# The order of TensorE's work inside a slot of a banded-attention and MLP kernel

## The chip, the cores and the metric

The kernel runs on one core of a Trainium2 chip. The metric is the device time of one execution in microseconds (us). Three runs of the kernel before took 751.92 to 752.27 us, median 752.23.

## What is computed

The reference, cut to what matters (x has 2048 rows of 512; 32 heads of 16 columns; window 256; hidden width 1792):

```python
x = A_x
xn = _layernorm(x, axis=-1)
# attention
qkv = (xn @ wqkv).reshape(B, S, 3, H, Dh).transpose(2, 0, 3, 1, 4)
scores = jnp.einsum("bhqd,bhkd->bhqk", q, k) * (Dh ** -0.5)
mask = (i - j >= 0) & (i - j < 256)
p = _softmax(jnp.where(mask, scores, -1e9), axis=-1)
s = jnp.einsum("bhqk,bhkd->bhqd", p, v).transpose(...).reshape(B, S, D) @ wo
# MLP
y = _layernorm(xn, axis=-1)
g = silu(gelu(y @ w1 + b1) @ w2 + b2)
return x + s * g
```

All of it is in float32. Each operand of a large product is split into a high and a low float32r part, and three matmuls (high times high, high times low, low times high) take the place of one.

## The kernel before

The attention works on groups of four heads (`NQ` = 8 groups) and on 16 blocks of 128 keys in each group. The loop at line 819 runs over slots t; slots 0 to 127 handle one (group, key block) each, slots -16 to -1 prepare the first group, and the MLP follows. In slot t the kernel runs four kinds of work for different blocks at once, and all of TensorE's instructions stand in the order in which the loop writes them (`keep_in_program_order`; the same holds for VectorE, ScalarE and GpSimd).

- **Scores** of the slot's key block: `prob_block(n, kb, p)` (line 548), once for p = 1, which I call the first scores, and once for p = 0, the second scores. Two matmuls write up to 384 columns for two heads into the two banks of `stb`, which exists once. ScalarE takes the exponential of both banks into a tile `pt`, and GpSimd masks its two triangles (`affine_select`). The next scores can be written only when ScalarE has read the banks.
- **Maxima** of block m = t + 12 (`LEAD`): `max_block` (line 496). Four matmuls write the scores of a query block against two key blocks into `xy`. VectorE lays, by the triangular mask, the scores of the block two further back (in `zo`) over the upper triangles (`copy_predicated`), and takes the maximum (`tensor_reduce`).
- **First-block scores**: `first_scores` (line 487), the four matmuls into `zo` that this mask copy reads. With `ahead=True` in `max_block` they were issued in the slot before.
- **Values**: `pv_step(n, qb)` (line 569), up to 24 small matmuls of the probabilities of the slot before into `otb`, a part of one bank of `zo`, and ScalarE's copy of it into `oraw` (`outs["copy"]`).
- **Fills**: `fill_in(t, half)` (line 812) runs the units that are planned for the first half (0) or the second half (1) of the slot. They are projections for later groups and the first hidden units of the MLP. `tandem` (line 440) spreads two such products over slots t0 to t1: each unit is a pair of matmuls on the upper and the lower 64 rows into the two banks `fb`. In the middle the banks change rows; the first unit after that waits, by a manual dependency, for the latest `outs["copy"]`. At slot t1 ScalarE copies one bank and VectorE the other. `places` puts up to a third of the product's units of a slot into the first half (4 of 12 pairs of 512 columns, 8 of 24 of 256), what is over into the second half, and up to 3 (or 6) last ones into the first half of t1. `BEHIND` (line 438) lists eight t1 whose ScalarE copy is issued in the second half.

The loop's order for TensorE, and with it for all engines, is in lines 825 to 846: first scores, maxima, first-half fills, the plan's other steps, second scores, second-half fills, first-block scores of the next slot, values. The `plan` (`at`) and the `ends` (`behind`) of a slot carry the splits of weights, layernorm steps and DMA issues. SyncE issues all DMAs, in program order.

"Slot" below means a turn of this loop. VectorE's chain in a slot is mask copy, then maximum; the next block's four matmuls into `xy` must wait for that maximum. The mask copy also waits in the program for ScalarE's latest copy of `otb`, which lies in the same bank as `zo`.

Of the kernel before, what the change touches and what calls it, by code (L numbers as in the profile page):

```python
# [23 lines left out]
NQ = H // 4  # L24
EPS = 1e-5
NEG = -3.0e38
LEAD = 12
# [23 lines left out]
def mixer_kernel(ctx, tc, x, wqk, wv, wo, w1, b1, w2, b2, out):  # L51


    nc = SimpleNamespace(**{name: Ordered(tc, name) for name in ("tensor", "vector", "scalar", "gpsimd", "sync")})
# [105 lines left out]
    def run(steps):  # L160
        for step in steps:
            step()
# [13 lines left out]
    def open_slot(i):  # L176
        slots.append(bigp.tile([P, 2, 2, S], F32R, tag=f"qk{i}", name=f"qk{i}"))
# [18 lines left out]
    fb = [psf.tile([P, 512], F32, name=f"fb{i}") for i in range(2)]  # L196
# [90 lines left out]
    now = [0, 0]  # L287
    delayed = {}
    fills = {}

    def later(k, fn):

        if k == 0:
            fn()
        else:
            h = 2 * now[0] + now[1] + k
            delayed.setdefault((h // 2, h % 2), []).append(fn)
# [137 lines left out]
                behind(t, nc.sync.dma_start, h_d[f - 6], raw)  # L435
        return 3 * KT, mm, finish

    BEHIND = (19, 24, 35, 41, 58, 74, 90, 104)

    def tandem(t0, t1, one, two, mid=None, back=None):  # L440

        n = one[0]
        lo, hi = slice(0, 64), slice(64, P)
        mid = mid or max(1, (t0 + t1 + 1) // 2)
        most = n // 4

        def places(slots, last):

            last = min(most, n // (len(slots) + 1)) if last else 0
            cuts = [(n - last) * k // len(slots) for k in range(len(slots) + 1)]
            out = []
            for t, a, b in zip(slots, cuts, cuts[1:]):
                ahead = min(b - a, max(n // 3, (b - a + 1) // 2))
                out += [(t, 0)] * ahead + [(t, 1)] * (b - a - ahead)
            return out + [(t1, 0)] * last

        first, second = places(range(t0, mid), False), places(range(back or mid, t1), True)
        for phase, where in enumerate((first, second)):  # L460
            for i in range(n):
                flags = dict(start=(phase == 0 and i == 0), stop=(phase == 1 and i == n - 1), skip_group_check=True)
                def unit(i=i, phase=phase, flags=flags):
                    made = ((two if phase == 0 else one)[1](fb[1 - phase], i, hi, **flags),
                            (one if phase == 0 else two)[1](fb[phase], i, lo, **flags))
                    if phase == 1 and i == 0:
                        for r in made:
                            tc.add_manual_dep(r.ins, outs["copy"].ins.name, ORDER, reason="the banks change rows")
                fills.setdefault(where[i], []).append((unit, ()))
        fills.setdefault((t1, int(t1 in BEHIND)), []).append((one[2], (fb[0], t1, nc.scalar.copy)))  # L470
        fills[t1, 0].append((two[2], (fb[1], t1, nc.vector.tensor_copy)))

    def spread(jobs, places):
# [13 lines left out]
    def first_scores(n, qb):  # L487

        slot = slots[n % 2]
        for p in range(2):  # L490
            for a in (1, 0):
                r = slice(64 * a, 64 * a + 64)
                nc.tensor.matmul(zo[:, a, P * p: P * (p + 1)], slot[r, 0, p, P * qb: P * (qb + 1)],
                                 slot[r, 1, p, P * (qb - 2): P * (qb - 1)], start=True, stop=True)

    def max_block(n, qb, ahead=False):

        slot = slots[n % 2]
        if qb % 4 == 0:
            mts[n, qb // 4] = small.tile([P, 2, 2, 4], F32, tag="mt", name=f"mt_{n}_{qb}")  # L500
        lo = max(qb - 1, 0)
        off = 128 * (lo + 1 - qb)
        for p in range(2):
            for a in (1, 0):
                r = slice(64 * a, 64 * a + 64)
                nc.tensor.matmul(xy[:, a, 256 * p + off: 256 * (p + 1)], slot[r, 0, p, P * qb: P * (qb + 1)],
                                 slot[r, 1, p, P * lo: P * (qb + 1)], start=True, stop=True)
        if qb >= 2 and not ahead:
            first_scores(n, qb)
        four = xy.rearrange("q a (p k) -> q a p k", p=2)  # L510
        nc.vector.copy_predicated(four[:, :, :, 128:256], mask,
                                  neg if qb < 2 else zo[:, :, 0:256].rearrange("q a (p k) -> q a p k", p=2))
        nc.vector.tensor_reduce(out=mts[n, qb // 4][:, :, :, qb % 4],
                                in_=four[:, :, :, off:256],
                                axis=AX.X, op=ALU.max, negate=True)
# [32 lines left out]
    def prob_block(n, kb, p):  # L548
        slot = slots[n % 2]
        w = min(384, S - P * kb)  # L550
        pt = pp.tile([P, 2, 384], F32, tag="pt", name=f"pt_{n}_{kb}_{p}")
        both = xy if p and 16 * n + kb + LEAD >= 16 * NQ else stb[0]
        for a in (1, 0):
            r = slice(64 * a, 64 * a + 64)
            nc.tensor.matmul(both[:, a, 0:w], slot[r, 1, p, P * kb: P * (kb + 1)],
                             slot[r, 0, p, P * kb: P * kb + w], start=True, stop=True)
        nc.scalar.activation(pt[:, :, 0:w], both[:, :, 0:w], AF.Exp, scale=DH ** -0.5)
        nc.gpsimd.affine_select(out=pt[:, :, 0:P], in_=pt[:, :, 0:P], pattern=[[0, 2], [1, P]],
                                compare_op=ALU.is_ge, fill=0.0, base=0, channel_multiplier=-1)
        if w == 384:  # L560
            nc.gpsimd.affine_select(out=pt[:, :, 256:384], in_=pt[:, :, 256:384],
                                    pattern=[[0, 2], [-1, P]], compare_op=ALU.is_gt, fill=0.0,
                                    base=0, channel_multiplier=1)
        pts[(n, kb, p)] = pt
# [4 lines left out]
    def pv_step(n, qb):  # L569

        lo = max(qb - 2, 0)
        for kb in range(lo, qb + 1):
            for j in range(4):
                nc.tensor.matmul(otb[32 * j: 32 * j + DH + 1], vt[:, kb, (4 * n + j) % 16],
                                 pts[n, kb, j // 2][:, j % 2, P * (qb - kb): P * (qb - kb + 1)],
                                 start=(kb == lo), stop=(kb == qb),
                                 skip_group_check=True, tile_position=(0, 32 * j))
        if qb % 4 == 0:
            outs[0] = sgp.tile([P, 512], F32, tag="or", name=f"oraw_{n}_{qb}", bufs=2)
        outs["copy"] = nc.scalar.copy(outs[0][:, P * (qb % 4): P * (qb % 4 + 1)], otb)  # L580
        if qb % 4 == 3:
            (at if n or qb > 7 else behind)(16 * n + qb + 2, nc.sync.dma_start, oT_d[n // 2, n % 2::2, :, P * (qb - 3): P * (qb + 1)], outs[0])
# [82 lines left out]
    def at(t, fn, *args):  # L665
        plan.setdefault(t, []).append((fn, args))
# [145 lines left out]
    def fill_in(t, half):  # L812
        now[:] = t, half
        run(delayed.pop((t, half), ()))
        for fn, args in fills.get((t, half), ()):
            fn(*args)

    end = 16 * NQ
    for t in range(-16, end + 1):
        m = t + LEAD  # L820
        if t == -5:
            open_slot(1)
            for k in range(4):
                at(-4 + k, clear_part, k)
        if 0 <= t < end:
            if t == 0:
                early.close()
                stb.append(attn.enter_context(tc.tile_pool(name="ps_s2", bufs=1, space=PSUM)).tile(
                    [P, 2, 512], F32, name="stb"))
            prob_block(t // 16, t % 16, 1)  # L830
        if t >= 0 and m < end:
            max_block(m // 16, m % 16, t > 0)
        fill_in(t, 0)
        for fn, args in plan.get(t, []):
            fn(*args)
        if 4 <= m < LEAD:
            max_block(0, m)
        if 0 <= t < end:
            prob_block(t // 16, t % 16, 0)
        fill_in(t, 1)  # L840
        if 0 <= m < 4:
            max_block(0, m)
        if t >= 0 and m + 1 < end and (m + 1) % 16 >= 2:
            first_scores((m + 1) // 16, (m + 1) % 16)
        if t >= 1:
            pv_step((t - 1) // 16, (t - 1) % 16)
        run(lns.get(t, ()))
        if 0 <= m < end and m % 4 == 3:
            max_rows(m // 16, m % 16 // 4, t)
        for fn, args in ends.get(t, []):  # L850
            fn(*args)
# [22 lines left out]
    for f in range(6, NF, 2):  # L874
        t = gp.tile([P, 2, 512], F32, tag="ohl", name=f"hr_{f}", bufs=4)
# [429 lines left out]
```

## Time and profile before

| what | value |
|---|---|
| median of three runs | 752.23 us |
| the profiled execution | 751.99 us |
| its span, first to last instruction | 750.3 us |
| TensorE busy | 735.8 us (98%) |
| VectorE, ScalarE, GpSimd busy | 511.3, 439.5, 299.1 us |
| slots 0 to 127 | about 62 to 427 us of the span |
| granted TensorE clock | 0.999 |

In the profile PE is TensorE's matmuls and PEld its weight loads, which may run beside matmuls; DVE is VectorE, ACT ScalarE, POOL GpSimd, SP SyncE. A row of the timeline gives start and duration in us, engine, line, operation, output <- inputs, shape, and in brackets the idle time before it with what ended it. All operations go through one recording helper and so have the line L43; they are told apart by their tiles. A matmul's duration includes the latency of the array, so busy times of PE say little about how close it is to its peak; the distance from one start to the next says more.

### The profile page before, as it was taken

What the parts mean: (1) busy time and instruction counts of PE and PEld (TensorE: products, weight loads), DVE (VectorE), ACT (ScalarE), POOL (GpSimd) and SP (SyncE); (2) the same over time, 40 slices, a digit from 0 to 9 for tenths busy, and PEclk for the clock granted to TensorE, in tenths of its full rate; (3) what the DMA queues carried; (4) which work ended last, traced back from release to release, by engine and by line L of the source; (5) the groups of instructions that cost most, each with busy time, mean ns of one, the idle gap of its engine ahead of it and who ended that gap; (6) DMA issues with size and microseconds to landing.
All of it is one profiled execution on the core that took longest, in us unless ns stands there. A gap on an engine that the chain in (4) does not pass through costs nothing.

```text
span 750.3 us, 18757 instructions
## 1 busy us (share of the span) xinstructions
PE 735.8 (98%) x7408; PEld 589.3 (79%) x7408; DVE 511.3 (68%) x781; ACT 439.5 (59%) x746; POOL 299.1 (40%) x644
## 2 busy tenths in 40 slices
PE   8999999999999999999999999999999999999997
PEld 7886777777778887777776688888888888888886
DVE  7886767877766778887772547763666765676643
ACT  7757767867667676778877745544453743442001
POOL 7413757767666555767866600120102000001102
PEclk9999999999999999999999999999999999999999
DMA  8633355766555535647734482542013332254711
GB/s 287 191 74 78 84 132 148 210 153 187 150 142 148 143 93 139 168 109 189 200 86 146 120 294 92 177 147 78 35 43 98 94 103 71 70 167 129 214 53 56
DMA packets 56951, 99.40 MB, mean 132 GB/s; under 512 B 11104, under 2 KB 11360, under 8 KB 56864
## 3 DMA queue, kind: packets, MB, share of 16 engines
q1 hardware_dynamic: 56864, 98.21, 46.0%
q8 instruction: 58, 0.95, 0.5%
q14 instruction: 29, 0.24, 0.1%
HBM read 51.39 MB, written 29.62 MB: 108 GB/s over the span
## 4 chain that ended last, share of the span: by engine, by line
PE 90%; ACT 4%; DVE 3%; DMA 1%; issue 1%; POOL 0%; SPq 0%; DVEq 0%; ACTq 0%
PE acc L43 20%; PE fb L43 19%; PE zo L43 12%; PE stb L43 9%; PE p L43 9%; PE s L43 6%; PE h L43 6%; PE xy L43 5%; PE pv L43 3%; ACT pt L43 3%; DVE xy L43 1%; PE yt L43 1%; DVE mt L43 1%; DMA qk<-pjr 0%; DMA x<-in_x_dram 0%
## 5 line engine op out<-in xcount | busy, mean ns | idle before, releaser
L43 POOL TENSOR_SCALAR_AFFINE_SELECT pt<-pt 128x256 f32<-128x256 f32 x480 | 193.7, 427 | 134.2 <-ACT pt L43 131.9
L43 ACT ACTIVATE pt<-stb 128x768 f32<-128x768 f32 (+1 forms) x244 | 188.4, 772 | 58.4 <-PE stb L43 51.7
L43 DVE TENSOR_REDUCE mt<-xy 128x4 f32<-128x1024 f32 (+1 forms) x128 | 152.6, 1192 | 4.4
L43 DVE COPY_PREDICATED xy<-upper,zo 128x512 f32<-128x512 int32 x112 | 77.8, 694 | 71.5 <-PE xy L43 64.9
L43 PE MATMUL fb<-xnT,wqb 64*128 64x512 f32 (+1 forms) x684 | 106.9, 398 | 0.3
L43 POOL TENSOR_TENSOR xo<-xo,gated 128x512 f32<-128x512 f32 x15 | 20.3, 1354 | 216.6 <-DVE gated L43 191.5
L43 PE MATMUL zo<-pt,vt 128*17 128x128 f32 x2880 | 103.7, 275 | 0.1
L43 PE MATMUL stb<-qk 64*128 64x384 f32 (+1 forms) x488 | 98.9, 401 | 4.5 <-ACT pt L43 2.8
L43 PE MATMUL acc<-w,gh 128*128 128x512 f32 x320 | 98.9, 390 | 0.0
L43 PEld LDWEIGHTS stb<-qk 64*128 64x128 f32 x488 | 45.5, 183 | 53.3 <-ACT pt L43 45.1
L43 PEld LDWEIGHTS zo<-pt,vt 128*17 128x17 f32 x2880 | 67.5, 97 | 15.2 <-issue 6.5
L43 PEld LDWEIGHTS fb<-xnT,wqb 64*128 64x128 f32 (+1 forms) x684 | 64.2, 185 | 10.0 <-DVE pjr L43 1.1
L43 PEld LDWEIGHTS acc<-w,gh 128*128 128x128 f32 x320 | 59.8, 188 | 12.1
L43 PE MATMUL acc<-w,gl 128*128 128x512 f32 x160 | 62.4, 390 | 0.0
L43 PE MATMUL xy<-qk 64*128 64x256 f32 (+2 forms) x536 | 58.3, 291 | 0.2 <-DVE mt L43 0.2
L43 ACT COPY oraw<-zo 128x128 f32<-128x128 f32 x128 | 34.2, 267 | 35.9 <-PE zo L43 34.8
L43 PEld LDWEIGHTS xy<-qk 64*128 64x128 f32 x536 | 46.8, 185 | 6.5 <-issue 3.1
L43 ACT ACTIVATE gated<-acc 128x512 f32<-128x512 f32 x16 | 8.7, 596 | 64.8 <-DVE acc L43 64.8
L43 PE MATMUL s<-wos,ohl 128*128 128x512 f32 (+1 forms) x204 | 44.7, 377 | 0.0
L43 PEld LDWEIGHTS zo<-qk 64*128 64x128 f32 x448 | 38.4, 185 | 6.0 <-issue 2.5
L43 PEld LDWEIGHTS s<-wos,ohl 128*128 128x128 f32 x204 | 36.7, 188 | 7.0
L43 ACT COPY p<-p 128x512 f32<-128x512 f32 x21 | 12.3, 584 | 49.5 <-PE p L43 42.2
(195 smaller groups left out, 1243.2 us busy)
## 6 DMA issues: line engine op xcount, KB each, us to landing
qk<-sh SPq DMA_DIRECT2D x128, 128.0 KB
qk<-pjr SPq DMA_DIRECT2D x64, 128.0 KB
oT_d<-oraw SPq DMA_DIRECT2D x32, 256.0 KB
w_d<-in_w_dram SPq DMA_DIRECT2D x14, 512.0 KB
x<-in_x_dram SPq DMA_DIRECT2D x16, 256.0 KB
or<-oT_d SPq DMA_DIRECT2D x16, 256.0 KB
w<-rden_d SPq DMA_DIRECT2D x16, 256.0 KB
xo<-in_x_dram SPq DMA_DIRECT2D x16, 256.0 KB
```

The source lines that it names most:

```text
L43: r = issue(*args, **kwargs)
```

## The change

The order inside a slot becomes: maxima, first scores, first-half fills, the plan's steps, first-block scores of the next slot, second scores, second-half fills, values. The first-block scores of blocks 12 and 24 are issued inside `max_block` (block 12 was before, too). `BEHIND` is removed, so each ScalarE copy of a bank stands in the first half of its slot t1. The manual dependency at the change of rows is kept only for products that begin before slot 116.

```diff
+    IN_PLACE = (LEAD, 24)
...
-    BEHIND = (19, 24, 35, 41, 58, 74, 90, 104)
...
-                    if phase == 1 and i == 0:
+                    if phase == 1 and i == 0 and t0 < 16 * NQ - LEAD:
                         for r in made:
                             tc.add_manual_dep(r.ins, outs["copy"].ins.name, ORDER, reason="the banks change rows")
...
-        fills.setdefault((t1, int(t1 in BEHIND)), []).append((one[2], (fb[0], t1, nc.scalar.copy)))
+        fills.setdefault((t1, 0), []).append((one[2], (fb[0], t1, nc.scalar.copy)))
...
+        if t >= 0 and m < end:
+            max_block(m // 16, m % 16, m not in IN_PLACE)
+        if 0 <= t < end:
             prob_block(t // 16, t % 16, 1)
-        if t >= 0 and m < end:
-            max_block(m // 16, m % 16, t > 0)
         fill_in(t, 0)
         for fn, args in plan.get(t, []):
             fn(*args)
         if 4 <= m < LEAD:
             max_block(0, m)
+        if t >= 0 and m + 1 < end and (m + 1) % 16 >= 2 and m + 1 not in IN_PLACE:
+            first_scores((m + 1) // 16, (m + 1) % 16)
         if 0 <= t < end:
             prob_block(t // 16, t % 16, 0)
         fill_in(t, 1)
         if 0 <= m < 4:
             max_block(0, m)
-        if t >= 0 and m + 1 < end and (m + 1) % 16 >= 2:
-            first_scores((m + 1) // 16, (m + 1) % 16)
         if t >= 1:
             pv_step((t - 1) // 16, (t - 1) % 16)
```

## The prediction

> **What bounds the kernel now.** I read the page first, then the waits, then the timeline of single slots.
>
> ```profile
> PE 735.8 (98%) x7408; PEld 589.3 (79%) x7408; DVE 511.3 (68%) x781; ACT 439.5 (59%) x746; POOL 299.1 (40%) x644
> PEld stb L43 <- ACT pt L43: 45.1, 161, 0.7
> ```
>
> 98% looks like a bound by TensorE, but the second row shows its weight load for the scores standing still 161 times until ScalarE has read `stb`. Slot 86 shows how. Its first scores are the `stb` before 312.09, its second scores are loaded at 313.39, and slot 87 begins at 314.74:
>
> ```profile
> 312.09 0.37 PEld L43 LDWEIGHTS xy<-qk 64*128 64x128 f32 x4
> 312.26 0.40 PE L43 MATMUL xy<-qk 64*128 64x256 f32 x4
> 312.50 1.11 PE L43 MATMUL fb<-xnT,wqb 64*128 64x512 f32 x8
> 312.52 0.81 ACT L43 ACTIVATE pt<-stb 128x768 f32<-128x768 f32 x1 [0.17 <-PE stb L43]
> 313.39 0.19 PEld L43 LDWEIGHTS stb<-qk 64*128 64x128 f32 x2 [0.23 <-ACT pt L43]
> ...
> 313.67 0.36 PE L43 MATMUL zo<-qk 64*128 64x128 f32 x4
> 313.88 0.81 ACT L43 ACTIVATE pt<-stb 128x768 f32<-128x768 f32 x1 [0.54 <-PE stb L43]
> 313.96 0.85 PE L43 MATMUL zo<-pt,vt 128*17 128x128 f32 x24
> 314.74 0.19 PEld L43 LDWEIGHTS stb<-qk 64*128 64x128 f32 x2 [0.21 <-ACT pt L43]
> 314.85 0.36 PEld L43 LDWEIGHTS xy<-qk 64*128 64x128 f32 x4
> 315.02 0.40 PE L43 MATMUL xy<-qk 64*128 64x256 f32 x4
> 315.26 1.08 PE L43 MATMUL fb<-xnT,wqb 64*128 64x512 f32 x8
> 315.29 0.81 ACT L43 ACTIVATE pt<-stb 128x768 f32<-128x768 f32 x1
> 315.52 0.70 DVE L43 COPY_PREDICATED xy<-upper,zo 128x512 f32<-128x512 int32 x1
> ```
>
> A weight load that found the array empty needs 0.11 us before its scores stream (314.74 to 314.85, when the next load is let in); the scores stream for 0.17 (314.85 to 315.02). I measure from streaming to streaming. First half: 312.09 to 313.50 (313.39 + 0.11) = 1.41. It is a round trip with ScalarE: 0.43 to the exponential at 312.52, 0.81 for it, 0.06 to the load at 313.39, 0.11. Second half: 313.50 to 314.85 = 1.35, likewise 0.38 + 0.81 + 0.05 + 0.11. The slot takes 2.76. TensorE's own work in each half nearly equals that, so the two loops are balanced, and what counts of the new order is which half gets longer.
>
> **The new order in an ordinary slot.** The second half loses `zo` and gains the next block's `xy`; the first half the reverse. The old trace has the new end of a slot at slot 118, where no maxima are left and values follow scores directly:
>
> ```profile
> 404.52 0.34 PE L43 MATMUL stb<-qk 64*128 64x384 f32 x2
> 404.78 0.85 PE L43 MATMUL zo<-pt,vt 128*17 128x128 f32 x24
> ```
>
> Scores to values is 0.26 (404.52 to 404.78). Values to the next load is 0.78 (313.96 to 314.74), its weights 0.11 (314.74 to 314.85), `xy` 0.24 (315.02 to 315.26). Sum 1.39, against ScalarE's trip of 1.35: TensorE becomes the bound of this half, by **+0.04**. In the first half TensorE needs 0.17 for the scores, 4 x 0.23 for the fills (322.01 to 322.24 below) and, for `zo`, I take 0.17 (two pairs of loads of 0.11 and 0.06, between 0.12 and 0.29, the step from 313.67 to 313.96): 1.26, under ScalarE's 1.41. The 0.15 of idle time there can't be lent to the other half, since ScalarE's trip, 1.41, and TensorE's 1.39 follow each other.
>
> Where the second half has a fill, TensorE bounds it already (slot 89, then slot 83, which has no `zo`):
>
> ```profile
> 322.01 0.39 PE L43 MATMUL fb<-xnT,wqb 64*128 64x512 f32 x2
> 322.24 0.33 PE L43 MATMUL zo<-qk 64*128 64x128 f32 x4
> 322.50 0.85 PE L43 MATMUL zo<-pt,vt 128*17 128x128 f32 x24
> ```
>
> ```profile
> 305.16 0.40 PE L43 MATMUL fb<-xnT,wqb 64*128 64x512 f32 x2
> 305.48 0.57 PEld L43 LDWEIGHTS zo<-pt,vt 128*17 128x17 f32 x24 [0.31 <-issue]
> ```
>
> Before, fill to `zo` to values takes 0.23 + 0.26 = 0.49. After, fill straight to values takes 0.32, and `xy` 0.24: 0.56, **+0.07**. By the plan, of slots 4 to 115 there are 48 ordinary ones with an empty second half and 25 with fills there: 48 x 0.04 + 25 x 0.07 = 3.7. Two more (20 and 52) have fills but no `zo` to lose, +0.23 each, and seven with short values or short maxima lose some 0.05 to 0.12: 0.9 together. The rest (1, 2 or 3 after a group's start, where values or maxima are short; the two slots with exponentials of 256 and 128 columns) I take at 0, since ScalarE or VectorE has the longer chain there. **+4.6** (0.02 to 0.05, and 0.05 to 0.09 each: 3.0 to 5.6).
>
> **New waits.** `zo` now stands in TensorE's queue ahead of the second scores, and it must wait for the mask copy, which starts 0.50 after `xy` (315.02 to 315.52) and takes 0.70: with 0.05 for the signal, 1.25 after `xy`, or 1.01 after the first scores. Weights of 0.11, 0.06, and 0.11 for the scores follow: 1.29, under 1.41. Margin 0.12. It is used up where VectorE has over a microsecond of other work between maximum and mask copy:
>
> ```profile
> 147.32 1.33 DVE L43 TENSOR_TENSOR wqb<-wqkr,wqb 128x512 fp32r<-128x512 f32 x1
> 149.42 0.30 PEld L43 LDWEIGHTS zo<-qk 64*128 64x128 f32 x4 [0.28 <-DVE xy L43]
> ```
>
> ```profile
> 176.33 0.68 DVE L43 TENSOR_TENSOR wqb<-wqkr,wqb 128x512 fp32r<-128x512 f32 x1
> ```
>
> Before, this cost slot 29 some 0.2 behind the second scores; now it holds them. With 1.33 + 0.2 of transpose in a gap of about 0.86, the copy is 0.7 late: +0.5 net. Slots 81 and 86 have similar, smaller cases. **+0.5** (0 to 1.6). The same subtraction takes 0.68 at 176.33. The Trainium skill (SBUF — State Buffer, Who interferes with whom) says that a VectorE instruction with two SBUF inputs contends with a GpSimd instruction that reads SBUF. By it, the 1.33 would go to 0.68, and the cost to 0, if the new timing took GpSimd's work away from under it; I see no reason for that.
>
> **The start.** In slot 0 `xy` and, in place, `zo` now precede the first scores:
>
> ```profile
> 61.00 1.23 DVE L43 TENSOR_REDUCE mt<-xy 128x4 f32<-128x1024 f32 x1
> 61.97 0.44 PE L43 MATMUL stb<-qk 64*128 64x384 f32 x2
> 62.28 0.51 PE L43 MATMUL xy<-qk 64*128 64x256 f32 x4
> ```
>
> `xy` waits until 62.23 for the maximum, so the scores leave at about 62.9 instead of 61.97. Later waits of slots 0 to 2 absorb half. **+0.4** (-0.4 to +0.9).
>
> **What is gained.** Banks: a product's first fills wait for VectorE's copy of its bank:
>
> ```profile
> 136.09 0.68 DVE L43 COPY pjr<-fb 128x512 f32<-128x512 f32 x1
> 136.51 0.40 PE L43 MATMUL xy<-qk 64*128 64x256 f32 x4
> 136.77 0.81 ACT L43 ACTIVATE pt<-stb 128x768 f32<-128x768 f32 x1
> 136.82 1.21 PE L43 MATMUL fb<-xnT,wqb 64*128 64x512 f32 x8
> 138.25 0.81 ACT L43 ACTIVATE pt<-stb 128x768 f32<-128x768 f32 x1 [0.16 <-PE stb L43]
> ```
>
> This first half takes 1.48 (136.77 to 138.25) instead of the 1.36 from 312.52 to 313.88. VectorE's chain begins 0.41 earlier against the scores, and the half's new idle 0.15 hides what remains. 15 such slots x 0.12: **-1.9** (-2.2 to -0.5). The moved ScalarE copies fit into the first half: 0.58 of copy in the 0.55 between two exponentials.
>
> Slot 11: `zo` for block 24 waits for a DMA.
>
> ```profile
> 96.88 0.33 PEld L43 LDWEIGHTS zo<-qk 64*128 64x128 f32 x4 [0.95 <-issue]
> ```
>
> In place in slot 12 it comes behind the values, 0.26 + 0.78 after the scores, when the data is there; it then adds 0.17. 0.95 - 0.17: **-0.8** (-1.0 to -0.3).
>
> The tail: two first units wait for `oraw`.
>
> ```profile
> 406.53 0.19 PEld L43 LDWEIGHTS fb<-yh,xnT 64*128 64x128 f32 x2 [0.67 <-ACT oraw L43]
> 420.85 0.19 PEld L43 LDWEIGHTS fb<-yh,xnT 64*128 64x128 f32 x2 [0.46 <-ACT oraw L43]
> ```
>
> The dropped dependency frees both: **-1.1** (-1.2 to -0.4; GpSimd's masks may be late next at the second).
>
> Slot 8: the cast that delays the exponential to 89.36 stands behind `oraw`, which comes earlier with the values by `zo`'s 0.26: **-0.2** (-0.3 to 0). DMA issues keep their order; what SyncE sends for the moved copies hangs on later steps.
>
> ```profile
> 88.68 0.27 ACT L43 COPY oraw<-zo 128x128 f32<-128x128 f32 x1 [0.17 <-PE zo L43]
> 88.84 0.62 ACT L43 CAST sh<-pjr 128x512 fp32r<-128x512 f32 x1
> ```
>
> **Sum.** 4.6 + 0.5 + 0.4 - 1.9 - 0.8 - 1.1 - 0.2 = +1.5 on the profiled execution's 751.99 (span 750.3, 1.7 around it): **753.5 us**. That execution lies 0.24 below the median, so against the median the forecast is +1.3, or 0.17%. About 0.2% (1.5 us) is what a measurement of this kernel can tell from no change; the forecast is just inside.
>
> **Rivals.**
> - *Slower: the mask copy decides.* The chain values, `oraw`, mask copy, `zo`, second scores becomes serial. Against it: the margin of 0.12. For it: some 40 slots hold a VectorE step of 0.68 or more ahead of the mask copy, and the copy also waits for `oraw`, whose 0.27 may be late behind other ScalarE work. The point: where the copy comes 0.12 late, each further tenth costs a tenth. At 0.2 late in 40 slots: 40 x 0.08 = 3.2, so 756.7. The Trainium skill (PSUM — Partial Sum Buffer, PSUM bank collisions raise a hardware error) says that two engines may not use one bank in one 32-partition quadrant at once, reads against reads too, which is why the copy must wait for `oraw`; that wait is the one priced here.
> - *Faster: the second half isn't TensorE's.* If values and `xy` pack more tightly than the rows of slot 118, the 4.6 is gone and only savings remain: 753.5 - 4.6 = 748.9. For it: the loads' 0.21 to 0.23 of idle time in slot 86. Against it: 0.20 of this follows every group of values, whether ScalarE is done or not.
> - *The copies don't come earlier:* if the first fills still wait as before, the -1.9 is gone: 755.4.
>
> **Chances.** Forecast (within 0.2%, 750.7 to 753.7) 0.46. Slower by more 0.40: mask copy 0.25, late banks or a larger price per slot 0.15. Faster by more 0.14. With all terms at their lower bounds the sum is -2.1, at their upper bounds about +7. The range takes 750.4 to 756.8: it holds the first and third rivals (756.7, 755.4) and leaves out the second (748.9) and the case of both slower rivals at once, together 2 in 10.
>
> **What would show it.** Right: second halves of slots such as 86 run 0.04 longer from exponential to exponential, first halves stay at 1.36, the wait of `stb` for ScalarE falls in the second half; slot 11 loses its second of waiting; no `fb` waits for `oraw` at the end; `zo` waits often for VectorE without holding the second scores. Wrong: first halves over 1.41, weight loads of `zo` waiting for VectorE over 0.2 us in many slots (first rival), or second halves that don't grow (second).

## The result and the profile after

The changed kernel takes 755.41 us (median of 5, 754.98 to 755.98), the kernel before 752.23 us (751.92 to 752.86, measured beside it): ratio 1.0041, interval 1.0026 to 1.0056. It is slower by 3.2 us. The forecast was 753.5 us, which is +1.5 on the profiled execution and +1.3 against the median, with a range of 750.4 to 756.8. The profiled execution took 754.98 us, its span is 753.3 us against 750.3: 3.0 us to be found in the two traces. (One of the two executions of experiment 5 below took 1753.84 us and one of the three of the kernel before beside it 878.68; these two slow runs are left out.)

First from the page of the kernel before, three groups of weight loads (busy time, mean ns, then the idle time before them and what ended most of it); then from the page of the changed kernel the busy times and the same three groups:

```profile
L43 PEld LDWEIGHTS stb<-qk 64*128 64x128 f32 x488 | 45.5, 183 | 53.3 <-ACT pt L43 45.1
...
L43 PEld LDWEIGHTS xy<-qk 64*128 64x128 f32 x536 | 46.8, 185 | 6.5 <-issue 3.1
...
L43 PEld LDWEIGHTS zo<-qk 64*128 64x128 f32 x448 | 38.4, 185 | 6.0 <-issue 2.5
```

```profile
PE 740.5 (98%) x7408; PEld 584.4 (78%) x7408; DVE 511.6 (68%) x781; ACT 440.8 (59%) x746; POOL 295.0 (39%) x644
...
L43 PEld LDWEIGHTS xy<-qk 64*128 64x128 f32 x536 | 40.4, 184 | 32.2 <-DVE mt L43 15.6
...
L43 PEld LDWEIGHTS stb<-qk 64*128 64x128 f32 x488 | 45.9, 184 | 10.6 <-ACT pt L43 8.6
L43 PEld LDWEIGHTS zo<-qk 64*128 64x128 f32 x448 | 35.3, 185 | 18.6 <-DVE xy L43 15.4
```

The scores hardly wait for ScalarE any longer: 8.6 us in place of 45.1. A reader of this row alone would expect a faster kernel. The idle time has gone to `xy` (32.2 in place of 6.5) and `zo` (18.6 in place of 6.0), which now stand in front of the scores, and to the loads of the values (29.0 in place of 15.2 on the two pages). What ended the idle time before `xy` is given as VectorE's maximum, but most of it is the 0.21 that follows every group of values. The same holds for a part of the old 45.1: of the 161 waits 67, with 19.0 us, stand directly behind values.

The timeline of slot 25 shows an ordinary slot, and also a half in which banks change hands (the prediction showed the first half of this slot before):

```profile
137.00 0.68 DVE L43 COPY pjr<-fb 128x512 f32<-128x512 f32 x1
...
137.67 0.34 PE L43 MATMUL stb<-qk 64*128 64x384 f32 x2
...
137.85 1.09 PE L43 MATMUL fb<-xnT,wqb 64*128 64x512 f32 x8
137.94 0.70 DVE L43 COPY_PREDICATED xy<-upper,zo 128x512 f32<-128x512 int32 x1
138.13 0.81 ACT L43 ACTIVATE pt<-stb 128x768 f32<-128x768 f32 x1 [0.40 <-PE stb L43]
...
138.68 0.30 PEld L43 LDWEIGHTS zo<-qk 64*128 64x128 f32 x4 [0.17 <-DVE xy L43]
...
139.00 0.44 PE L43 MATMUL stb<-qk 64*128 64x384 f32 x2
...
139.37 0.85 PE L43 MATMUL zo<-pt,vt 128*17 128x128 f32 x24
139.49 0.81 ACT L43 ACTIVATE pt<-stb 128x768 f32<-128x768 f32 x1
140.15 0.30 PEld L43 LDWEIGHTS xy<-qk 64*128 64x128 f32 x4 [0.21 <-DVE mt L43]
```

```profile
140.50 0.34 PE L43 MATMUL stb<-qk 64*128 64x384 f32 x2
...
140.94 0.81 ACT L43 ACTIVATE pt<-stb 128x768 f32<-128x768 f32 x1 [0.38 <-PE stb L43]
```

First half: 138.13 to 139.49, 1.36, where it took 1.48; the fills run without a break, 1.09 instead of 1.21. Second half: 139.49 to 140.94, 1.45, where an ordinary one took 1.41. From streaming to streaming it is 139.11 (139.00 and 0.11 of loading) to 140.50, 1.39, the very sum of the prediction, and no load of scores waits for ScalarE in it.

Where zo holds the scores, slots 28 and 29:

```profile
148.18 1.28 POOL L43 TENSOR_TENSOR pjr<-pjr,sh 128x512 fp32r<-128x512 f32 x1
148.23 1.78 DVE L43 TENSOR_TENSOR wqb<-wqkr,wqb 128x512 fp32r<-128x512 f32 x1
...
150.07 0.66 DVE L43 COPY_PREDICATED xy<-upper,zo 128x512 f32<-128x512 int32 x1
...
150.78 0.30 PEld L43 LDWEIGHTS zo<-qk 64*128 64x128 f32 x4 [1.01 <-DVE xy L43]
...
151.49 0.81 ACT L43 ACTIVATE pt<-stb 128x768 f32<-128x768 f32 x1 [1.27 <-PE stb L43]
```

The subtraction now takes 1.78 instead of 1.33, the mask copy comes at 150.07, `zo` stands 1.01 in the queue and the exponential of the second scores comes 0.74 late.

Slots 3 and 4, which the prediction did not speak of:

```profile
75.29 0.33 PEld L43 LDWEIGHTS xy<-qk 64*128 64x128 f32 x4 [0.91 <-DVE mt L43]
75.33 0.44 PE L43 MATMUL xy<-qk 64*128 64x128 f32 x4 [0.65 <-DMA qk<-pjr]
...
75.57 0.42 PE L43 MATMUL stb<-qk 64*128 64x384 f32 x2
```

Block 16 is the first of the second group; its operands come by a DMA. In the old order the same matmuls stood behind the first scores; now the scores stand behind them and wait, too. The second half of slot 3 takes 2.15 instead of 1.41.

The two first units of the tail no longer stand idle (no bracket; they waited 0.67 and 0.46):

```profile
409.97 0.19 PEld L43 LDWEIGHTS fb<-yh,xnT 64*128 64x128 f32 x2
```

```profile
423.80 0.19 PEld L43 LDWEIGHTS fb<-yh,xnT 64*128 64x128 f32 x2
```

I measured every half of every slot from exponential to exponential in both traces. The differences, after less before:

| term | predicted | traces |
|---|---|---|
| second halves of slots 4 to 115, apart from the rows below | +4.6 | +5.6 |
| first halves there, the four late ones left out (banks) | -1.9 | -2.7 |
| late `zo`: first halves of slots 17, 29, 86, 93 | +0.5 | +1.7 (0.31, 0.74, 0.39, 0.29) |
| start: up to slot 2 | +0.4 | +0.4 |
| slot 3, waiting for block 16's operands | none | +0.75 |
| slot 11 | -0.8 | -0.5 |
| tail: slots 116, 119, 125 | -1.1 | -1.4 |
| slot 8 | -0.2 | -0.2 |
| second halves of slots 80, 91, 92, 107, 115 | none | -0.7 |
| sum | +1.5 | +3.0 |

Of the last row, 0.13 belongs to slot 107 and to that one execution: its second half took 1.60 there and 1.43 to 1.45 in the other kernels with the old order. The row of the start is less certain than it looks, too. Slots 0 to 2 take 9.65 to 9.67 with the old order and 9.21 to 9.22 with the new one in every trace (experiments 5 and 6, which change these slots, aside), 0.45 less. But the exponential of slot 0 begins 0.86 later here, at 63.36 against 62.50, and in the traces of the experiments with the old order it begins anywhere from 62.2 to 63.1, with the new order from 63.0 to 63.4. By the means of the two orders the start costs some 0.2, not 0.4.

### The profile page after: what moved, and what is told of

It reads as the page before. It is cut to its first block, busy times and chain, and to the rows that moved or that the text cites. A ratio compares the mean times of both kernels' runs of the same rounds, so it can differ in the third digit from the quotient of the medians.

```text
span 753.3 us, 18760 instructions
## 1 busy us (share of the span) xinstructions
PE 740.5 (98%) x7408; PEld 584.4 (78%) x7408; DVE 511.6 (68%) x781; ACT 440.8 (59%) x746; POOL 295.0 (39%) x644
## 4 chain that ended last, share of the span: by engine, by line
PE 86%; issue 5%; DVE 3%; ACT 2%; POOL 2%; DMA 1%; ACTq 0%; DVEq 0%; SPq 0%; POOLq 0%
PE acc L43 20%; PE fb L43 15%; PE zo L43 14%; PE p L43 9%; PE xy L43 7%; PE stb L43 7%; PE s L43 6%; PE h L43 6%; POOL pt L43 1%; ACT pt L43 1%; DVE xy L43 1%; PE pv L43 1%; DVE mt L43 1%; PE yt L43 1%; ACT x L43 1%
## 5 line engine op out<-in xcount | busy, mean ns | idle before, releaser
L43 POOL TENSOR_SCALAR_AFFINE_SELECT pt<-pt 128x256 f32<-128x256 f32 x480 | 189.1, 418 | 142.1 <-ACT pt L43 139.6
L43 PE MATMUL stb<-qk 64*128 64x384 f32 (+1 forms) x488 | 92.0, 373 | 1.9 <-ACT pt L43 1.4
L43 PEld LDWEIGHTS fb<-xnT,wqb 64*128 64x128 f32 (+1 forms) x684 | 66.1, 185 | 10.0 <-issue 1.1
L43 PE MATMUL xy<-qk 64*128 64x256 f32 (+2 forms) x536 | 69.1, 332 | 1.7 <-DVE mt L43 1.0
L43 PEld LDWEIGHTS xy<-qk 64*128 64x128 f32 x536 | 40.4, 184 | 32.2 <-DVE mt L43 15.6
L43 PEld LDWEIGHTS zo<-qk 64*128 64x128 f32 x448 | 35.3, 185 | 18.6 <-DVE xy L43 15.4
L43 PE MATMUL zo<-qk 64*128 64x128 f32 x448 | 40.9, 260 | 1.3 <-DVE xy L43 0.8
```

The lines of the kernel that those rows point to most:

```text
L43: r = issue(*args, **kwargs)
```

## The experiments

The theory to be tested: TensorE's price in the second halves, plus the cases in which what now stands ahead of the scores waits itself, outweigh what the banks and the tail save. The rivals: the moved ScalarE copies freed the banks; the mask copy decides in every slot; the second half has room left; the savings need the new order. All differences of halves below are read from the traces.

**1. The tail's dependency alone.**

```diff
-                    if phase == 1 and i == 0:
+                    if phase == 1 and i == 0 and t0 < 16 * NQ - LEAD:
```

> The kernel before with one part of the change alone: no manual dependency at the change of rows for products that begin at slot 116 or later. Theory (the dependency itself is the wait): the first halves of slots 119 and 125 lose 0.71 and 0.48, as between the two traces, nothing else moves, 1.2 us less: 751.0 us. Rival (the units were free only because the new order finishes the values earlier): below 0.3 us less, and the two loads of fb still wait for oraw.

Slots 119 and 125 lose 0.71 and 0.47, as in the changed kernel. The median is 751.55 against 752.17, ratio 0.9989 (0.9980 to 0.9998): 0.6 us, not 1.2. In the trace, two things that the edit doesn't touch came out longer: the exponential of slot 0 began 0.59 later, and slot 11 took 2.96 instead of 2.39, since the DMA that it waits for landed later. Whether such things explain the half that is missing in the timed runs stays open. The wait was the dependency's, and the rival falls.

**2. The ScalarE copies alone.**

```diff
-    BEHIND = (19, 24, 35, 41, 58, 74, 90, 104)
+    BEHIND = ()
```

> The kernel before with BEHIND empty and nothing else, so all ScalarE copies of banks stand in the first half. Theory (the bank waits went because VectorE's copy comes earlier against the scores in the new order): the first fills still wait after slots 20, 25, 36, 42, 59, 75, 105, and the time is the same within 0.3 us. Rival (the moved ScalarE copies free the banks): about 8 slots gain 0.12, 1.0 us less.

752.37 against 752.17, ratio 1.0002 (0.9993 to 1.0010): nothing. The first half of slot 20, in the timeline of this kernel, still has the broken row of fills:

```profile
122.40 0.81 ACT L43 ACTIVATE pt<-stb 128x768 f32<-128x768 f32 x1 [0.37 <-PE stb L43]
...
122.51 1.17 PE L43 MATMUL fb<-xnT,wqb 64*128 64x512 f32 x8
...
123.89 0.81 ACT L43 ACTIVATE pt<-stb 128x768 f32<-128x768 f32 x1 [0.16 <-PE stb L43]
```

1.49, as before. So the moved copies alone do not free the banks. In the changed kernel slots 54, 64 and 99 lose 0.13 to 0.15 as well, and the copies of their banks were in the first half already: there the order did it without a moved copy. (The new order with the old places of the eight copies was not run.)

**3. Maxima of block 16 in their old place.** In the changed kernel:

```diff
-        if t >= 0 and m < end:
+        if t >= 0 and m < end and m != 16:
             max_block(m // 16, m % 16, m not in IN_PLACE)
         if 0 <= t < end:
             prob_block(t // 16, t % 16, 1)
+        if m == 16:
+            max_block(1, 0, True)
```

> The changed kernel, but the maxima of block 16 (slot 4, the first of the second group) behind the first scores of that slot, as before. Theory (their operands come by a DMA that lands after the new place, and the first scores queue behind them): the second half of slot 3 goes from 2.15 back to about 1.41, 0.7 us less, 754.6 us. Rival (VectorE's maximum of slot 3 holds them, or the DMA holds the slot at any place): the 0.7 moves into slot 4 and the time stays.

754.62, ratio to the kernel before 1.0034 (1.0022 to 1.0047); the changed kernel's was 1.0041. The second half of slot 3 goes from 2.15 to 1.41, but the first half of slot 4 from 1.35 to 1.62:

```profile
74.81 0.44 PE L43 MATMUL stb<-qk 64*128 64x384 f32 x2
75.32 0.33 PEld L43 LDWEIGHTS xy<-qk 64*128 64x128 f32 x4 [0.33 <-issue]
...
76.97 0.81 ACT L43 ACTIVATE pt<-stb 128x768 f32<-128x768 f32 x1 [0.81 <-PE stb L43]
```

`xy` still stands idle for 0.33 before it is loaded, and the fills behind it come late; but the first scores have gone ahead, and ScalarE works meanwhile. Of 0.75 some 0.28 remains (0.45 less net in the trace), so the truth lay between theory and rival.

**4. The split of slot 28 in slot 27.**

```diff
-    for n, t in enumerate((-5, 5, 16, 28, 38, 70, 80), 1):
-        at(t - 4, fetch_wqk, n)
+    for n, t in enumerate((-5, 5, 16, 27, 38, 70, 80), 1):
+        at(24 if t == 27 else t - 4, fetch_wqk, n)
```

> The changed kernel, but the split of a weight that stands in slot 28 (ScalarE cast, VectorE subtraction) made in slot 27. Theory (the subtraction of 1.78 us makes the next mask copy late, and zo holds the second scores of slot 29): the first half of slot 29 goes from 2.09 to 1.35 to 1.45; how much is left depends on slot 28, whose mask copy now comes behind the subtraction: it keeps 0 if the subtraction takes 0.7 without GpSimd's work beside it, and up to 0.6 if it takes over 1.3. So 0 to 0.6 us less. Rival (not VectorE's lateness but the order of slot 29 itself): slot 29 keeps its 2.09.

754.69, ratio to the kernel before 1.0033 (1.0021 to 1.0045). Slot 29's first half falls from 2.09 to 1.35, as the theory says. Away from GpSimd's subtraction, VectorE's takes 0.68:

```profile
145.38 0.68 DVE L43 TENSOR_TENSOR wqb<-wqkr,wqb 128x512 fp32r<-128x512 f32 x1
```

But slot 27's first half grows from 1.35 to 1.74, for a reason that I had not thought of, in ScalarE's queue:

```profile
143.68 0.81 ACT L43 ACTIVATE pt<-stb 128x768 f32<-128x768 f32 x1 [0.37 <-PE stb L43]
144.39 0.61 ACT L43 CAST wqb<-wqkr 128x512 fp32r<-128x512 f32 x1
144.90 0.62 ACT L43 CAST sh<-pjr 128x512 fp32r<-128x512 f32 x1
145.42 0.81 ACT L43 ACTIVATE pt<-stb 128x768 f32<-128x768 f32 x1
```

Between the exponentials of a first half there is room for one such cast, and slot 27 had one already.

**5. Only zo moved** (the kernel before, with these lines from behind the second-half fills to before the second scores):

```diff
+        if t >= 0 and m + 1 < end and (m + 1) % 16 >= 2:
+            first_scores((m + 1) // 16, (m + 1) % 16)
         if 0 <= t < end:
             prob_block(t // 16, t % 16, 0)
```

> The kernel before with one of the two moves alone: zo in front of the second scores, maxima still behind the first scores. Theory (zo waits for the mask copy, 1.25 after xy, and xy now streams 0.17 after the first scores): zo streams 1.42 after the first scores, then 0.17 for it and 0.11 for the scores' weights: first halves of 1.70 instead of 1.41 in the 83 or so slots that have zo, +0.29 each, less 0.1 in some 30 slots with fills in the second half: 20 to 25 us more, about 774 us. Rival (the mask copy has room anywhere in the half): same time or up to 3 us less.

772.9 us in one execution, the profiled one; its span is 771.2. Slot 38 shows the chain of the first rival at work:

```profile
179.60 0.44 PE L43 MATMUL stb<-qk 64*128 64x384 f32 x2
...
179.88 0.40 PE L43 MATMUL xy<-qk 64*128 64x256 f32 x4
...
180.38 0.70 DVE L43 COPY_PREDICATED xy<-upper,zo 128x512 f32<-128x512 int32 x1 [0.93 <-PE xy L43]
...
181.13 0.30 PEld L43 LDWEIGHTS zo<-qk 64*128 64x128 f32 x4 [0.35 <-DVE xy L43]
...
181.41 0.39 PE L43 MATMUL stb<-qk 64*128 64x384 f32 x2
```

0.50 to the mask copy, 0.75 for it and its signal, then `zo` and the scores: 179.71 to 181.41 is 1.70, as worked out. Ordinary first halves take 1.68 instead of 1.35, +0.33. So moving the maxima ahead is what pays for moving `zo`: with it, ordinary first halves stay at 1.35, and the margin of 0.12 that was worked out for them is not used up.

**6. Only the maxima moved** (the changed kernel with `first_scores` back behind the second-half fills):

```diff
-        if t >= 0 and m + 1 < end and (m + 1) % 16 >= 2 and m + 1 not in IN_PLACE:
-            first_scores((m + 1) // 16, (m + 1) % 16)
         if 0 <= t < end:
             prob_block(t // 16, t % 16, 0)
```

> The changed kernel with zo behind the second scores, as before, and maxima in front: the other move alone. Theory (TensorE bounds the second half): scores to zo 0.24, zo to values 0.29, values to the next load 0.78, 0.11, xy 0.24: 1.66, so second halves 0.21 to 0.25 longer than in the changed kernel in some 85 slots, +19; slots 17, 29, 86 and 93 get back 1.7: 770 to 774 us. Rival (the second half still has room, ScalarE bounds it): within 2 us of the changed kernel.

766.98 us (two executions), ratio 1.0200 (1.0156 to 1.0244), below the 770 to 774 that I expected. Second halves are 0.17 longer than in the changed kernel; I had said 0.21 to 0.25. Slot 26:

```profile
144.62 0.44 PE L43 MATMUL stb<-qk 64*128 64x384 f32 x2
...
144.90 0.33 PE L43 MATMUL zo<-qk 64*128 64x128 f32 x4
...
145.16 0.85 PE L43 MATMUL zo<-pt,vt 128*17 128x128 f32 x24
```

From the scores' load to values it is 0.54; without `zo` it was 0.37 (139.00 to 139.37 above). The difference, 0.17, is what the second halves grew by: these four matmuls are paid in full there. Slots 17, 29, 86 and 93 have first halves of 1.35 again, so their lateness was `zo`'s wait.

**7 and 8. Less work in the second half, in both orders.**

```diff
-        lo = max(qb - 2, 0)
+        lo = max(qb - 1, 0)
```

> The changed kernel, values summed over two key blocks instead of three (8 of 24 small matmuls left out in nearly every slot). Theory (TensorE bounds the second half by 0.04): ordinary second halves go from 1.45 to ScalarE's 1.41 and no further, though 0.2 of TensorE's work has gone; those with one pair of fills lose 0.2. Rival (the maxima at the slot's start wait for VectorE's maximum): ordinary second halves keep 1.45.

> The kernel before, values summed over two key blocks instead of three. Theory (ScalarE bounds the ordinary second half): those keep 1.41, those with fills lose 0.2 each; against the changed kernel with the same cut, ordinary second halves come out equal, and the changed kernel is slower by 1 to 1.5 us instead of 3. Rival (TensorE bounds the half before, too): ordinary second halves shrink by some 0.05 or more.

Both kernels leave out the third key block of the values, so they compute something else than the reference; they serve only to free time on TensorE. 742.53 us in the new order (ratio to the full kernel before 0.9875, 0.9832 to 0.9917), 743.43 in the old (0.9887, 0.9844 to 0.9929), of two executions each; the spans are 740.9 and 742.0. With short values the new order is the faster one, by 0.9 to 1.1 us; I had expected it to stay slower by 1 to 1.5. In the trace of the old order 0.66 of this is one stall, scores of slot 38 that wait for a DMA (`qk<-mT_d`); without it the two are within half a microsecond. The halves are as the theory says. Slot 26, new order, then old:

```profile
140.18 0.81 ACT L43 ACTIVATE pt<-stb 128x768 f32<-128x768 f32 x1
...
141.04 0.19 PEld L43 LDWEIGHTS stb<-qk 64*128 64x128 f32 x2
...
141.58 0.81 ACT L43 ACTIVATE pt<-stb 128x768 f32<-128x768 f32 x1 [0.44 <-PE stb L43]
```

```profile
138.72 0.81 ACT L43 ACTIVATE pt<-stb 128x768 f32<-128x768 f32 x1
...
139.58 0.19 PEld L43 LDWEIGHTS stb<-qk 64*128 64x128 f32 x2 [0.45 <-ACT pt L43]
...
140.13 0.81 ACT L43 ACTIVATE pt<-stb 128x768 f32<-128x768 f32 x1 [0.39 <-PE stb L43]
```

1.40 and 1.41, where the full kernels have 1.45 and 1.41 (slots 25 and 86 above and in the prediction). In the old order the load of the scores now stands idle for 0.45, twice its 0.23, and the half did not get shorter; in the new order the half gave back its 0.04 and no more of the 0.2, and the scores are loaded at 141.04, 0.05 after the exponential's end (140.18 + 0.81). That is ScalarE's bound in both; in the full kernel the new order had TensorE's.

How far does this go? In the full kernels 87 second halves of slots 4 to 115 pay for the new order, 5.0 us together (not counting six at the end of a group, whose next first halves give it back). With short values 55 of them pay no longer (2.4 in the full kernels, 0.1 here, the stall left out). The other 32 hold fills, and TensorE stays the bound there: they still pay 2.1 instead of 2.5. So about half of the price is paid because the second half doesn't have 0.04 to 0.07 to spare. The rest of the turn comes mostly from elsewhere: the stall of slot 38, and slots 29 and 86, which are not late in this timing (1.1 together). The new order still pays 0.74 in slot 3 and 0.9 for late `zo` in slots 17 and 93.

**9. Both savings in the old order.** Experiment 1, and block 24 in place:

```diff
+    IN_PLACE = (24,)
...
-            max_block(m // 16, m % 16, t > 0)
+            max_block(m // 16, m % 16, t > 0 and m not in IN_PLACE)
...
-        if t >= 0 and m + 1 < end and (m + 1) % 16 >= 2:
+        if t >= 0 and m + 1 < end and (m + 1) % 16 >= 2 and m + 1 not in IN_PLACE:
```

> The kernel before without the manual dependency at slot 116 and later, and with the first-block scores of block 24 in slot 12 instead of slot 11 (old order everywhere). Theory (both savings of the changed kernel need no new order): slots 119 and 125 lose 1.2 together, the second half of slot 11 goes from 2.39 to about 1.41 and slot 12 grows by 0.17: 2.0 us less, 750.2 us. Rival (the DMA's landing is only moved into slot 12, which then waits as long): 751.0 to 751.5 us.

749.89 us, ratio 0.9970 (0.9958 to 0.9981): faster than both kernels, by 2.3 us than the kernel before. Slot 11 goes from 2.39 to 1.43, slot 12 grows by 0.27 (not 0.17), slots 119 and 125 lose 1.2. Since slot 11's wait differs from one trace to another (see experiment 1), so does what its removal saves.

**10. The same with a ninth pair of 256 columns in the first half.**

```diff
-                ahead = min(b - a, max(n // 3, (b - a + 1) // 2))
+                ahead = min(b - a, max(n // 3 + n // 24, (b - a + 1) // 2))
```

> As the kernel with both savings in the old order, and one more pair of 256 columns in the first half of the 14 slots that have such pairs in the second. Theory: the old first half has TensorE work of 0.17 + 0.24 + 8 x 0.117 = 1.35 under ScalarE's 1.41, so a ninth pair lengthens it by 0.05 to 0.06 and shortens the second half by 0.117: 14 x 0.06 = 0.8 us less than without it, 749.4 us. Rival (no room at all): first halves of those slots grow by 0.117 and nothing is gained.

750.38 us, ratio 0.9974 (0.9964 to 0.9984): no gain over the last. In ordinary slots the first half grows by 0.05 to 0.10 and the second shrinks by 0.09 to 0.13; where banks change (54, 59, 64) it is +0.12 and -0.12, and in slots 65 to 67 the second half gives back next to nothing. The old first half has less room than my sum of TensorE's durations said.

**11. The same edit in the changed kernel.**

> The changed kernel with the same ninth pair of 256 columns in the first half of those 14 slots. Theory (zo takes 0.17 where xy took 0.24, so the new first half has 0.15 of TensorE's time idle): first halves stay at 1.35, second halves lose 0.117: 14 x 0.117 = 1.6 us less, 753.8 us. Rival (the mask copy or TensorE already bounds the new first half): first halves grow by 0.1, no gain.

754.49 us, ratio 1.0032 (1.0019 to 1.0044). Second halves shrink by 0.12 as said in 12 of the 14 slots (by 0.08 in slot 65, by nothing in slot 66), but most first halves grow by 0.03 to 0.08 (1.35 to 1.38 or 1.43; slot 64 by 0.12). In the trace the 14 slots lose 0.7 together, not 1.6. (The span is 0.9 shorter, but 0.4 of that lies ahead of slot 0, which the edit doesn't touch.) The new first half had some 0.05 to 0.1 idle, not 0.15.

**12. Three amendments of the changed kernel together** (experiments 3, 4 and 11).

> The changed kernel with three amendments: maxima of block 16 behind the first scores, the split of slot 28 in slot 27, the ninth pair. If the three are independent: -0.45, -0.40 and -1.6: 753.0 us. That would still be above the kernel before, since the second halves keep TensorE's price of 0.04 to 0.07 in some 80 slots.

753.41 us, ratio 1.0016 (1.0008 to 1.0025). The span is 751.5, 1.8 less than the changed kernel's and about the sum of what the three did alone (0.4, 0.3 and 0.9). What remains is, as expected, in the second halves: those of slots 4 to 115 still take 2.8 more together than in the kernel before.

## Why the prediction was right, and where it was not

The measured time lies in the range, but not in the case that was held likeliest (within 0.2%, 0.46); it is the case slower by more (0.40). The forecast was right about the mechanism and the direction, and the size came out at twice what was said. That 755.4 is also the figure of the third rival is chance: its cause did not occur.

*The ordinary slot* was right to the hundredth: TensorE became the bound of the second half, 1.39 from stream to stream; 45 second halves grew by up to 0.05, 0.037 on average, and 38 by 0.05 to 0.085, 0.064 on average. Experiments 6 to 8 show that it is TensorE's work that is paid there. The term came out at 5.6 instead of 4.6, because it was counted too narrowly: many of the slots "1, 2 or 3 after a group's start" and those with short exponentials, which I took at 0, pay as well (six of the latter 0.12 each), and slots 67 and 83 pay 0.14 and 0.23 like 20 and 52. Part of it comes back in the first halves, -2.7 instead of -1.9, which was the banks' term; the two errors nearly cancel, which is luck.

*The new waits* are the step that failed. The prediction put them at "+0.5 (0 to 1.6)" and named slots 29, 81 and 86; the cost is 1.7, in slots 17, 29, 86 and 93, and slot 81 is not late. I took VectorE's durations from the old trace and moved only the places. But the subtraction grew with the move, from 1.33 to 1.78 in slot 28 and from 1.34 to 1.75 in slot 16, which made slot 17 late, too; the layernorm step ahead of slot 86's mask copy grew from 1.08 to 1.50 (it takes 0.54 in the changed kernel with short values, where slot 86 is not late); and slot 93's mask copy stands behind a subtraction of 0.69 and a transpose of 0.20 that wait for ScalarE first. Experiment 4 shows that slot 29's delay goes when the subtraction does, and experiment 6 that all four are `zo`'s wait.

*A wait not seen:* I looked for DMAs that `zo` waits for (slot 11) and not for those that `xy` waits for (block 16, +0.75). The question what a moved group waits for was asked of one of the two groups only, outside the start. Experiment 3 shows the cause; with the old place for that block 0.45 comes back.

*Slot 11* saved 0.5, not 0.8. The wait went, but `zo` in place was priced at 0.17, and in the new order the half takes 1.91, 0.46 more than an ordinary one: behind the values `zo` is loaded only when ScalarE's copy of them is done.

```profile
98.12 0.27 ACT L43 COPY oraw<-zo 128x128 f32<-128x128 f32 x1
98.44 0.30 PEld L43 LDWEIGHTS zo<-qk 64*128 64x128 f32 x4
```

In the old order the same step costs 0.27 (experiment 9). The saving is loose as well: the old half took 2.39, 2.90 and 2.96 in three kernels (the kernel before, experiments 2 and 1), as the DMA landed, and 1.91 to 1.92 in all with the new order that have full values. *The start* came out at the +0.4 of the forecast partly by luck, as said below the table. *The tail* was right (slots 119 and 125 lose 1.2; slot 116 loses 0.2 that was not forecast) and needs no new order (experiments 1 and 9).

*The rivals.* That the mask copy decides everywhere did not happen: its margin held in ordinary slots (a wait of 0.17 before `zo` in slot 25, and the second scores on time). The sign named for this rival, loads of `zo` that wait for VectorE over 0.2 us in many slots, did appear (25 times; 55 waits with 15.4 us in all), and yet no first half but these four grew by more than 0.08: a wait there costs nothing while ScalarE isn't done. The price, had the margin been used up, is 0.33 per slot (experiment 5). That the second half isn't TensorE's is refuted by experiments 6 to 8. That the copies don't come earlier is refuted by slot 25's unbroken fills, and experiment 2 shows that the moved ScalarE copies alone don't bring this.

## What to carry to other kernels

When two engines' loops are balanced, a row of waiting that falls from 45.1 to 8.6 us is no gain: count for each half what its longest chain is after the move, and multiply hundredths by the number of turns. Everything that is put ahead of a critical instruction in one queue brings its own waits along, so ask for each moved group, in its worst turns, what it waits for: a mask copy behind a long step, a DMA of a group's first block. And try the side edits of a reordering alone: here two of them, without the reordering, made the better kernel (749.89 us).

## What was unexpected of the hardware

VectorE's subtraction with both inputs in SBUF takes 0.68 with nothing of GpSimd's beside it (experiment 4), and no longer where GpSimd's step begins after it (slots 5, 38 and 70). Where GpSimd's subtraction of 1.28 had begun first, it took 1.33 with 0.78 of overlap (old order, slot 28) and 1.78 with 1.23 (new order): in both cases 0.55 more than the overlap, as if it stood still through nearly all of it. The old order's pair:

```profile
146.81 1.29 POOL L43 TENSOR_TENSOR pjr<-pjr,sh 128x512 fp32r<-128x512 f32 x1
147.32 1.33 DVE L43 TENSOR_TENSOR wqb<-wqkr,wqb 128x512 fp32r<-128x512 f32 x1
```

When VectorE begins first, it is GpSimd's that grows, to 1.57. From the changed kernel, slot 80:

```profile
300.35 0.68 DVE L43 TENSOR_TENSOR wqb<-wqkr,wqb 128x512 fp32r<-128x512 f32 x1
300.60 1.57 POOL L43 TENSOR_TENSOR pjr<-pjr,sh 128x512 fp32r<-128x512 f32 x1 [0.27 <-ACT sh L43]
```

The Trainium skill (SBUF — State Buffer, Who interferes with whom) says the same: such a pair contends, and issue order decides who blocks; the numbers here agree. I had weighed that rule only as a possible gain. In the changed kernel VectorE's subtraction of slot 28 began 0.05 after GpSimd's and took 1.78; in the same kernel with short values it began 0.12 ahead, took 0.70, and slot 29 was not late. So a shift of 0.17 in who begins first changed this duration by over a microsecond, and with it who is late.
